# Awaiting the output's landing on the scalar engine instead of the sync engine

## The chip, the cores and the metric

The kernel runs on one core of one Trainium2 chip. The metric is device time in microseconds (us). Every execution also leaves a profile, whose span runs from the first to the last instruction of the program. The time is longer than the span (420.02 against 418.7 us in the kernel before), and the trace still records updates of semaphores up to 1.42 us after the span's end.

Five engines have instruction streams of their own: tensor (PE), vector (DVE), scalar (ACT), GpSimd (POOL) and sync (SP, which starts the DMAs here: all 46 of the trace before). Of that trace's 11609 instructions PE has 10472 (with the weight loads), DVE 715, ACT 330, POOL 40 and SP 52. In this kernel they wait for one another through semaphores (sync, for one, 40.6 us for vector's last cast before it starts the output DMA).

## The reference, cut to what matters

One decoding step of a block: modulation of the input, grouped attention over a cache of 32,768 positions, a projection, then a small MLP. All weights and both caches have to be read from HBM (178.28 MB in the profile); the output is 2 x 1 x 1024 bf16, 4 KB.

```python
def reference(A_x, A_k_cache, A_v_cache, A_wq, A_wo, B_x, B_w1, B_b1, B_w2, B_b2, c, w_mod):
    # ... _A_ref: q = x @ wq; softmax(q k^T) v over the cache; @ wo
    # ... _B_ref: layernorm, w1, gelu, w2
    # ...
    h = _layernorm(x, axis=-1) * (1 + cb) + sb
    x = x + gb * _B_ref(h, B_w1, B_b1, B_w2, B_b2)
    return x
```

## The kernel before

The kernel records the operations of each engine with the semaphore waits that they need, and emits them in one block, one section for each engine. At the end of the block all engines meet in a closing barrier. The change and the argument touch only the last lines of the kernel:

```python
    # ... (the whole computation is recorded above)
    dve(lambda e: e.tensor_copy(res16[:, :], psM[0:16, 0:128]), reads=["psM"], writes=["res16", "c16"])

    s_out = nc.alloc_semaphore("s_out")
    T.wait("sp", reads=["res16"])
    T.raw("sp", lambda e: e.dma_start(out.rearrange("b o (k p) -> (b o k) p", p=128), res16[:, :]).then_inc(s_out, 16))

    with nc.Block(no_gpsimd_drain=True) as block:
        T.emit(block)              # the sections of the engines, then the closing barrier
    nc.sync.wait_ge(s_out, 16)     # behind the barrier: the output DMA has landed
```

The output DMA is started by sync inside the block, and sync waits for its sixteen increments behind the barrier, so that the barrier runs while the DMA is in flight (in the trace the barrier lets the engines go between 418.09 and 418.15 us, and the DMA's increments come from 418.53 to 418.69).

## Time and profile before

| | kernel before |
|---|---|
| time, median of 3 runs | 419.99 us (419.98 to 420.00) |
| span of the profiled run (its time) | 418.7 us (420.02) |
| read from HBM | 178.28 MB, 426 GB/s |

The page of the profile, cut to the lines that say what bounds the kernel (the DMA row gives the mean busy share of the DMA engines in tenths, in 40 equal slices of the span):

```profile
span 418.7 us, 11609 instructions
...
DMA  9989999999999999999999999999999999899995
...
HBM read 178.28 MB, written 0.00 MB: 426 GB/s over the span
## 4 chain that ended last, share of the span: by engine, by line
DMA 71%; PE 24%; DVE 2%; issue 1%; ACT 1%; SPq 1%
```

The DMA engines are busy to the end: 0.99 of the time up to 417.3 us. The change can't touch that; it touches what comes after. The same kernel in order of time, its last two microseconds (start, duration, engine, line, operation):

```profile
417.03 0.28 DVE L736 CAST c<-psM 16x128 bf16<-16x128 f32 x1 [0.37 <-PE psM L734]
417.34 0.35 SPq L740 DMA_DIRECT2D out_dram<-c  x1
```

And what sync's queue waited for, same kernel (line, releaser, us in total, times, longest):

```profile
SPq L740 <- DVE c L736: 40.6, 1, 40.6
...
SPq L744 <- DMA out_dram<-c: 0.6, 1, 0.6
SPq L742 <- PEq L742: 0.2, 1, 0.2
```

L742 is the closing barrier, L744 the wait behind it. The single instruction at L744, before (engine, operation, duration in ns, first and last start in us):

```profile
L744 SPq EVENT_SEMAPHORE  x1: 17/17/17, 418.7 to 418.7; - x1
```

Read together with the semaphore records of the trace (in us from the span's start): the cast ends at 417.31, sync has started the output DMA by 417.69, the barrier lets every engine go between 418.09 and 418.15, the DMA's last increment is recorded at 418.69, and sync's wait starts at 418.707 and ends at 418.724. That is the end of the span. So the last thing in the program is a wait of 0.6 us for a DMA in flight, with all other engines done.

### The profile page before, as it was taken

The numbers are of one execution on the slowest core, as the hardware profiler recorded it, in microseconds if no ns is written. First come the engines' busy times: TensorE is split into PE (matmuls) and PEld (weight loads), VectorE is DVE, ScalarE is ACT, GpSimd is POOL, SyncE is SP. The second block draws the span as 40 slices with busy tenths as digits, with TensorE's granted clock in tenths as the row PEclk, the third lists the DMA queues.
The fourth block names the chain that finished last, engine by engine and source line by source line (L and its number), as shares of the span: only waits on it lengthen the run. The fifth ranks groups of instructions, "written<-read, shape, count | busy, mean of one in ns | idle before, by whom it ended". The sixth has DMA issues, their size and how long they took to land.

```text
span 418.7 us, 11609 instructions
## 1 busy us (share of the span) xinstructions
PE 291.0 (70%) x5183; PEld 231.3 (55%) x5183; DVE 209.6 (50%) x423; ACT 149.4 (36%) x179; POOL 6.8 (2%) x29
## 2 busy tenths in 40 slices
PE   1407449766996895699369957976995699564536
PEld 1104219762993794299149926962894399221214
DVE  1201105546677676467726664766477567620411
ACT  2000015533565364256405632643365166400100
POOL 3000000000000000000000000000000000000000
PEclk9999557986896997799589958986697889576585
DMA  9989999999999999999999999999999999899995
GB/s 373 450 380 449 448 404 493 398 406 446 441 432 429 423 451 429 419 454 457 391 435 476 407 416 448 438 438 426 438 438 426 416 460 457 377 448 428 424 427 249
DMA packets 5581, 178.42 MB, mean 426 GB/s; under 512 B 698, under 2 KB 706, under 8 KB 964
## 3 DMA queue, kind: packets, MB, share of 16 engines
q1 hardware_dynamic: 5572, 178.28, 98.8%
q8 instruction: 8, 0.13, 0.1%
q14 instruction: 1, 0.01, 0.0%
HBM read 178.28 MB, written 0.00 MB: 426 GB/s over the span
## 4 chain that ended last, share of the span: by engine, by line
DMA 71%; PE 24%; DVE 2%; issue 1%; ACT 1%; SPq 1%
DMA V<-in_A_v_cache_dram 39%; DMA wo<-in_A_wo_dram 10%; DMA K<-in_A_k_cache_dram 10%; PE psZ L584 10%; DMA w<-in_B_w_dram 9%; PE psKT L536 8%; DMA wmod<-in_w_mod_dram 4%; PE psS L548 1%; PE psZ L548 1%; PE psS L655 1%; PE psZ L729 1%; PE psZ L469 1%; ACT KT_sb L540 0%; PE psS L469 0%; DVE m1c L553 0%
## 5 line engine op out<-in xcount | busy, mean ns | idle before, releaser
L536 PE MATMUL psKT<-ident,K 128*128 128x128 bf16 x2048 | 163.1, 229 | 11.5 <-DMA K<-in_A_k_cache_dram 11.5
L540 ACT ACTIVATE KT_sb<-psKT 128x1024 bf16<-128x1024 bf16 x96 | 98.2, 1025 | 124.4 <-PE psKT L536 124.4
L542 DVE COPY KT_sb<-psKT 128x1024 bf16<-128x1024 bf16 x160 | 106.7, 688 | 61.6 <-PE psKT L536 61.2
L536 PEld LDWEIGHTS psKT<-ident,K 128*128 128x128 bf16 x2048 | 126.7, 102 | 13.0 <-DMA K<-in_A_k_cache_dram 12.7
L584 PE MATMUL psZ<-V,E_sb 128*32 128x512 bf16 x512 | 46.4, 541 | 23.2 <-DMA V<-in_A_v_cache_dram 20.0
L548 PE MATMUL psS<-qcur,KT_sb 128*128 128x8 bf16 x1024 | 44.7, 167 | 2.2 <-issue 2.2
L584 PEld LDWEIGHTS psZ<-V,E_sb 128*32 128x32 bf16 x512 | 18.7, 130 | 47.7 <-issue 38.8
L548 PE MATMUL psZ<-qcur,KT_sb 128*128 128x8 bf16 x1024 | 43.0, 167 | 2.2 <-issue 1.5
L548 PEld LDWEIGHTS psS<-qcur,KT_sb 128*128 128x128 bf16 x1024 | 40.0, 97 | 2.3 <-issue 2.3
L548 PEld LDWEIGHTS psZ<-qcur,KT_sb 128*128 128x128 bf16 x1024 | 37.9, 96 | 3.4 <-issue 1.6
L572 ACT ACTIVATE E_sb<-S_sb 128x512 bf16<-128x512 f32 x32 | 19.5, 630 | 29.6 <-DVE S_sb L570 29.6
L570 DVE TENSOR_TENSOR S_sb<-S_sb,gmb 128x512 f32<-128x512 f32 x32 | 20.0, 685 | 0.3
L576 DVE TENSOR_REDUCE rs<-E_sb 128x8 f32<-128x512 bf16 x32 | 19.7, 675 | 0.0
L469 PE MATMUL psS<-wmod,inT 128*32 128x512 bf16 x32 | 5.1, 624 | 16.2 <-DMA wmod<-in_w_mod_dram 16.2
L553 DVE TENSOR_REDUCE m1c<-psZ 128x8 f32<-128x512 f32 x16 | 11.1, 693 | 10.2 <-ACT S_sb L552 10.1
L595 DVE RECIPROCAL rinv<-psM 128x1 f32<-128x1 f32 x8 | 1.3, 168 | 27.7 <-PE psM L593 27.7
L605 PE MATMUL psM<-msum,hmat 128*128 128x128 f32 x16 | 4.2, 347 | 13.3 <-DVE msum L600 13.3
L559 PE MATMUL psM<-identf,m 128*8 128x128 f32 x16 | 4.3, 369 | 13.1 <-DVE m L556 13.1
L553 DVE TENSOR_REDUCE m1c<-psS 128x8 f32<-128x512 f32 x16 | 11.1, 693 | 3.2 <-ACT S_sb L552 3.1
L552 ACT ACTIVATE S_sb<-psZ 128x512 f32<-128x512 f32 x16 | 9.5, 595 | 7.5 <-PE psZ L548 7.5
L477 DVE COPY S_sb<-psS 128x512 f32<-128x512 f32 x1 | 0.7, 690 | 22.9 <-PE psS L469 22.9
L469 PEld LDWEIGHTS psS<-wmod,inT 128*32 128x32 bf16 x32 | 1.1, 132 | 19.3 <-DMA wmod<-in_w_mod_dram 18.0
(123 smaller groups left out, 167.5 us busy)
## 6 DMA issues: line engine op xcount, KB each, us to landing
K<-in_A_k_cache_dram SPq DMA_DIRECT2D x16, 4096.0 KB, 27.1
wq<-in_A_wq_dram SPq DMA_DIRECT2D x2, 4096.0 KB, 44.8
wo<-in_A_wo_dram SPq DMA_DIRECT2D x2, 4096.0 KB, 39.0
w<-in_B_w_dram SPq DMA_DIRECT2D x2, 3584.0 KB, 32.5
wmod<-in_w_mod_dram SPq DMA_DIRECT2D x1, 6144.0 KB, 29.8
w<-in_B_w_dram SPq DMA_DIRECT2D x3, 2048.0 KB, 37.8
wmod<-in_w_mod_dram SPq DMA_DIRECT2D x1, 4608.0 KB, 15.8
wmod<-in_w_mod_dram SPq DMA_DIRECT2D x1, 1536.0 KB, 6.0
```

What stands on the lines that cost most here:

```text
L469: pe(lambda e, w=it.view, k=k, kk=kk, ch=ch, n=n, q=q: e.matmul(bank[n][32 * q:32 * q + 32, :], lhsT=inT[:, k, :], rhs=w[:, kk, ch * 512:( ...
L536: pe(lambda e, kq=kq, jj=jj, w=kt, t=t: e.transpose(psKT[kq][:, jj * 128:(jj + 1) * 128], w[:, t, :], ident[:, :]), reads=[it.reg, "ident" ...
L540: act(lambda e, src=src: e.activation(KT_sb[g8][:, :, :], src, ACT.Copy), reads=[f"psKT{kq}"], writes=[f"KT_sb{g8}"], sem=f"ev{cc}_{g8}")
L542: dve(lambda e, src=src: e.tensor_copy(KT_sb[g8][:, :, :], src), reads=[f"psKT{kq}"], writes=[f"KT_sb{g8}"], sem=f"ev{cc}_{g8}")
L548: pe(lambda e, t=t, jj=jj: e.matmul(ps[:, t * HPG:(t + 1) * HPG], lhsT=KT_sb[g8][:, jj, :], rhs=qcur[:, :], start=True, stop=True), reads= ...
L552: act(lambda e: e.activation(Sc, ps.rearrange("p (t h) -> p h t", h=HPG), ACT.Copy), reads=[preg], writes=[f"S_sb_{cc}"], sem=f"sc{cc}")
L553: dve(lambda e: e.tensor_reduce(m1c[:, :, cc], ps.rearrange("p (t h) -> p h t", h=HPG), AX.X, ALU.max), reads=[preg], writes=[f"m1c{cc}"])
L559: pe(lambda e: e.matmul(psM[0:HPG, 0:128], lhsT=m1[:, :], rhs=identf[:, :], start=True, stop=True), reads=["m1", "identf"], writes=["psM"])
L570: dve(lambda e: e.tensor_tensor(Sc, Sc, gmb[:, :].unsqueeze(2).to_broadcast([128, HPG, TPC]), ALU.subtract), reads=[f"S_sb_{cc}", "gmb"], ...
L572: act(lambda e: e.activation(Ec, Sc.rearrange("p h (u t) -> p u h t", t=4), ACT.Exp, scale=SCALE), reads=[f"S_sb_{cc}"], writes=[f"E_sb_{c ...
L576: dve(lambda e: e.tensor_reduce(rs4[:, :, cc], Ec.rearrange("p u h t -> p h u t"), AX.XY, ALU.add), reads=[f"E_sb_{cc}"], writes=[f"rs4_{c ...
L584: pe(lambda e, t4=t4, tg=tg, q=q: e.matmul(psO[32 * q:32 * q + 32, :], lhsT=E_sb[:, tg // 4, :, :].rearrange("p h t -> p (h t)"), rhs=vt[: ...
```

## The change

The wait for the output is moved to another engine. It stays behind the barrier; the DMA, its issuer and its semaphore stay. The intent can be read as taking the wait from the engine that has just started the DMA and giving it to one that has been idle for 16 us.

```diff
     with nc.Block(no_gpsimd_drain=True) as block:
         T.emit(block)
-    nc.sync.wait_ge(s_out, 16)
+    nc.scalar.wait_ge(s_out, 16)
```

## The prediction

In the recorded texts a serpentine is a row of nine increments of one semaphore, taken as a walk through the five engines and back, and the postamble is what follows the program's last instruction. The trace's records hold the time of an update and the number of its semaphore, not the value and not the engine: which update is an increment, which a reset, and which engine makes it, is my reading, which the runs with other waiters test.

> **What bounds the kernel now.** Memory traffic, not the tail. The profile's page has a span of 418.7 us with DMA at 9 tenths in nearly every slice, 426 GB/s on average, and a chain that ended last of 71% DMA and 24% PE. The change touches only the last microsecond. There the trace, in order of time, has: DVE's last cast ends at 417.31; the sync engine issues the output DMA from 417.34 to 417.69; the closing barrier (semaphore instructions at L742) releases every engine between 418.09 and 418.15; the output DMA's sixteen increments arrive from 418.53 to 418.69; sync's wait at L744 starts at 418.707 and takes 17 ns. So sync really waits 0.6 us (the view of waits says the same), all of it the DMA's flight.
>
> **What the change removes, adds, moves.** One wait (17 ns) leaves sync's stream and one enters the scalar engine's. Scalar's last work is the sigmoid at 402.24, and the barrier releases it when it releases sync. The DMA, its issuer and its semaphore stay, so the wait should again end at about 418.72. Span: 418.7 within 0.1.
>
> [...] The profiled run's time, 420.02, is 1.30 us longer than its span. The trace's semaphore-update records show what follows the kernel: nine increments of one semaphore (418.387, .421, .631, .676, .841, .885, .923, .957, 419.004), then resets of all semaphores in five runs until 419.56, then nine increments again until 420.14. [...] From the order of the reset runs I read sync as the turning point, reached last on the way up, and scalar as the second. In the kernel before, four increments are made while sync still waits (the fifth at 418.841, 117 ns after the wait's end). With scalar held instead, only the first is early; the third, fourth and fifth, hidden before, come after scalar's. Estimate from the undisturbed serpentine at the trace's end (323 ns from second increment to ninth): scalar leaves its wait at 418.72, takes 117 ns (as sync) to at most 311 ns (its bound now) to its increment, and 323 ns later the ninth falls at 419.17 to 419.36 instead of 419.004. That is +0.16 to +0.35 us (0.04 to 0.08%), all on the critical path, since resets and the second serpentine follow.
>
> **Prediction.** 420.2 us, 8 times in 10 between 419.6 and 420.9. Chances: faster by over 2%: 0.01; within 2%: 0.98; slower by over 2%: 0.01.
>
> **What would show each step.** The wait stands on scalar and ends within 20 ns of the last increment; the span stays at 418.7 within 0.1; time minus span grows from 1.30 to about 1.5 us; the second increment (not the fifth) comes after 418.72, the rest follow at about 40 ns. The stream (426 GB/s, 71% DMA) is unchanged.
>
> **What would make it wrong.** If scalar is at the serpentine's turn, the effect is zero or slightly negative. If scalar's path from its last instruction into the postamble is longer than 311 ns once it starts late, the loss is larger. If two builds differ in the 418.7 us of traffic by a few tenths, that hides the effect; the three runs of before agree within 0.02 us, but are one build.

## The result, and the profile after

| | before | after |
|---|---|---|
| time, median of 6 runs | 420.01 us (419.98 to 420.09) | 420.32 us (420.26 to 420.40) |
| time, mean of the 6 | 420.023 | 420.323 |
| profiled run: time / span, from the trace | 420.02 / 418.724 | 420.29 / 418.749 |
| time minus span of the profiled run | 1.296 | 1.541 |

The ratio of the two kernels is 1.0007, 95% interval 0.9994 to 1.002. At a threshold of 2% the two kernels are the same, and the interval includes 1. Yet all six runs of after lie above all six of before, by 0.30 us in the mean. The page after:

```profile
span 418.7 us, 11609 instructions
...
DMA  9989999999999999999899999999999999899995
...
HBM read 178.28 MB, written 0.00 MB: 426 GB/s over the span
## 4 chain that ended last, share of the span: by engine, by line
DMA 79%; PE 18%; issue 1%; DVE 1%; SPq 1%; ACT 1%
```

The stream is the same. The chain's split is not (79% DMA instead of 71%), though nothing before the last microsecond was changed and the span is the same: in the kernel before it follows mostly matmuls from 104.9 to 138.0 us, and after the change a transfer from 100.1 to 130.4 us. A change in its shares alone proves nothing. In order of time, after:

```profile
417.05 0.28 DVE L736 CAST c<-psM 16x128 bf16<-16x128 f32 x1 [0.37 <-PE psM L734]
417.36 0.35 SPq L740 DMA_DIRECT2D out_dram<-c  x1
```

What sync's queue waited for, after; the wait at L744 is gone from it:

```profile
SPq L740 <- DVE c L736: 40.5, 1, 40.5
...
SPq L742 <- PEq L742: 0.2, 1, 0.2
```

And the instruction at L744, after, now on scalar's queue:

```profile
L744 ACTq EVENT_SEMAPHORE  x1: 17/17/17, 418.7 to 418.7; - x1
```

The last increment of the DMA is at 418.711, scalar's wait at 418.732 to 418.749. Up to here the two kernels differ by 0.025 us, and the wait itself costs 17 ns on either engine. The time came after the span, where the views of the profile show nothing; the trace's records of semaphore updates do. This is what they hold of one semaphore (number 2, which no instruction of the program names), in us from the end of the last wait (the span's end), so that the traces can be laid over each other:

```
first row of nine        1      2      3      4      5      6      7      8      9
before (sync held)   -0.337 -0.303 -0.093 -0.048 +0.117 +0.161 +0.199 +0.233 +0.280
after (scalar held)  -0.341 +0.125 +0.163 +0.207 +0.231 +0.336 +0.376 +0.411 +0.457

second row of nine      10     11     12     13     14     15     16     17     18
before               +1.062 +1.097 +1.135 +1.178 +1.202 +1.301 +1.339 +1.373 +1.420
after                +1.243 +1.346 +1.384 +1.428 +1.451 +1.550 +1.588 +1.622 +1.669
```

In between, from 0.12 us after the fifth increment in both traces, come single updates of semaphores numbered 7 to 255 in five rising runs (226 records from 418.961 to 419.562 us before, 245 from 419.095 to 419.768 after), which I read as resets. Two things grew. In the first row, only one increment instead of four is made while the wait lasts, and the ninth comes 0.177 us later (0.457 - 0.280). In the second row, the eleventh follows the tenth after 0.103 us instead of 0.035, which adds another 0.07. Together the eighteenth comes 0.249 us later, and time minus span grew by 0.245.

### The profile page after: what moved, and what is told of

Its sections match the earlier page's. It is cut to its first block, busy times and chain, and to the rows that moved or that the text cites. A ratio compares the mean times of both kernels' runs of the same rounds, so it can differ in the third digit from the quotient of the medians.

```text
span 418.7 us, 11609 instructions
## 1 busy us (share of the span) xinstructions
PE 290.7 (69%) x5183; PEld 231.0 (55%) x5183; DVE 209.7 (50%) x423; ACT 149.4 (36%) x179; POOL 6.8 (2%) x29
## 4 chain that ended last, share of the span: by engine, by line
DMA 79%; PE 18%; issue 1%; DVE 1%; SPq 1%; ACT 1%
DMA V<-in_A_v_cache_dram 46%; DMA K<-in_A_k_cache_dram 10%; DMA wo<-in_A_wo_dram 10%; PE psZ L584 10%; DMA w<-in_B_w_dram 9%; PE psKT L536 4%; DMA wmod<-in_w_mod_dram 4%; PE psS L655 1%; PE psS L548 1%; PE psZ L729 1%; PE psZ L548 1%; PE psZ L469 1%; PE psS L469 0%; SPq L647 0%; ACT KT_sb L540 0%
## 5 line engine op out<-in xcount | busy, mean ns | idle before, releaser
L655 PE MATMUL psS<-wo,atT 128*32 128x512 bf16 x64 | 7.0, 614 | 8.3 <-DMA wo<-in_A_wo_dram 8.3
L477 DVE COPY S_sb<-psS 128x512 f32<-128x512 f32 x1 | 0.7, 691 | 23.0 <-PE psS L469 23.0
L664 DVE COPY S_sb<-psS 128x512 f32<-128x512 f32 x2 | 1.4, 691 | 21.6 <-PE psS L655 14.6
```

Source lines behind the costliest of these rows:

```text
L655: pe(lambda e, w=it.view, m=m, j=j, hf=hf, q=q: e.matmul(psS[0][32 * q:32 * q + 32, :], lhsT=atT[m][:, j, :], rhs=w[:, j, hf * 512:(hf + 1 ...
```

## The experiments

The theory is that nine increments are a walk through the five engines and back, in a fixed order. A held engine early in the order delays more of the walk. There are four rivals: A, sync should hold the wait; B, chance differences between builds; C, scalar alone is slow to leave a wait; D, an instruction more in scalar's stream costs, held or not.

The differences are some tenths of a microsecond of 420. At the threshold of 2% every run is the same as the kernel before, and only w_pool, in_sp and in_act have a 95% interval of the ratio that lies above 1. Two finer measures are used: the traces' increments as above, and the mean of time minus span over all runs (spans are listed to 0.1 us, so one value is good to 0.05). For the kernel before that mean was 1.30, 1.29 and 1.30 in the three sets of runs below, each on one chip (9, 9 and 7 runs). All runs were correct.

| run | waits behind the barrier | median us (before, same set) | time minus span, mean | increment 9 | gap 10 to 11 | increment 18 |
|---|---|---|---|---|---|---|
| before (profiled) | sync | - | 1.30 | +0.280 | 0.035 | +1.420 |
| after | scalar | 420.32 (420.01) | 1.54 | +0.457 | 0.103 | +1.669 |
| both | sync and scalar | 420.33 (420.08) | 1.55 | +0.456 | 0.119 | +1.687 |
| w_dve | vector | 420.27 (420.08) | 1.43 | +0.402 | 0.034 | +1.546 |
| w_pe | tensor | 420.43 (420.08) | 1.60 | +0.564 | 0.034 | +1.704 |
| w_pool | GpSimd | 420.72 (420.08) | 1.88 | +0.831 | 0.034 | +1.974 |
| w_act | scalar | 420.25 (420.05) | 1.55 | +0.457 | 0.108 | +1.675 |
| idle_act | sync; scalar's is fulfilled | 420.12 (420.05) | 1.38 | +0.279 | 0.115 | +1.500 |
| in_sp | sync's is fulfilled | 420.91 (420.05) | 1.76 | +0.746 | 0.034 | +1.888 |
| in_act | scalar's is fulfilled | 421.09 (420.05) | 1.84 | +0.734 | 0.107 | +1.950 |
| idle4 | sync; scalar's are fulfilled | 420.34 (420.16) | 1.50 | +0.280 | 0.034 | +1.410 |
| idle8 | sync; scalar's are fulfilled | 420.09 (420.16) | 1.33 | +0.294 | 0.034 | +1.435 |
| idle_in | sync | 420.32 (420.16) | 1.51 | +0.279 | 0.034 | +1.415 |
| act_m1 | scalar | 420.47 (420.16) | 1.63 | +0.457 | 0.034 | +1.723 |

### Which engine is held: both, w_dve, w_pe, w_pool

```diff
# both                                # w_dve
     nc.sync.wait_ge(s_out, 16)      -    nc.sync.wait_ge(s_out, 16)
+    nc.scalar.wait_ge(s_out, 16)    +    nc.vector.wait_ge(s_out, 16)
# w_pe                                # w_pool
-    nc.sync.wait_ge(s_out, 16)      -    nc.sync.wait_ge(s_out, 16)
+    nc.tensor.wait_ge(s_out, 16)    +    nc.gpsimd.wait_ge(s_out, 16)
```

Expected of both:

> The wait on the output stands on the sync engine and on the scalar engine. Theory ([...] scalar is second, sync fifth): the earlier engine in the order decides, so this is the changed kernel again: time 0.25 to 0.35 us over the kernel before, second increment at about 0.125 us after the scalar wait's end, ninth at about 0.46 us after it. Rival A (the sync engine should be kept busy or the move itself, fewer instructions on sync, costs): within 0.1 us of the kernel before. Rival B (chance difference between two builds): anything within 0.3 us.

Expected of w_dve:

> The wait stands on the vector engine alone. Theory: vector is fourth in the serpentine, so only sync's hop and the turn come after it: increments 1 to 3 early, the fourth about 0.12 us after the wait's end, the ninth about 0.37 us after it (0.12 + 0.024 + 0.105 + 0.040 + 0.035 + 0.046) against 0.28 in the kernel before and 0.457 in the changed one: time +0.09 us over the kernel before, 0.05 to 0.2. Rival C (scalar alone is slow to leave a wait): within 0.05 us of the kernel before.

Expected of w_pe:

> The wait stands on the tensor engine alone. Theory: tensor is first, so no increment at all before the wait's end; its own path from its last instruction to its increment is 0.235 us in both traces, then 0.034 to scalar and 0.332 from scalar's to the ninth: ninth about 0.60 us after the wait's end, time +0.32 to 0.45 us over the kernel before (its wait instruction takes 51 ns, not 17). Rival C: within 0.05 us of the kernel before.

Expected of w_pool:

> The wait stands on GpSimd alone. Theory: third in the order, but its own path from its last instruction to its increment was 0.567 us in the kernel before (it came last of the first four there), so increments 1 and 2 early, third about 0.567 us after the wait's end, ninth about 0.86 us after it: time +0.5 to 0.65 us over the kernel before. If position alone counts and not the path: +0.15 us. Rival C: within 0.05 us.

Each wait stands where it was meant to. The instruction in w_dve, w_pe and w_pool, in this order (PEldq and DVEq are the queues of tensor and vector):

```profile
L744 DVEq EVENT_SEMAPHORE  x1: 21/21/21, 418.8 to 418.8; - x1
```

```profile
L744 PEldq EVENT_SEMAPHORE  x1: 51/51/51, 418.8 to 418.8; - x1
```

```profile
L744 POOLq EVENT_SEMAPHORE  x1: 17/17/17, 418.9 to 418.9; - x1
```

The first row of increments in their traces, in us from the wait's end:

```
                   1      2      3      4      5      6      7      8      9
w_pe (tensor)   +0.198 +0.232 +0.270 +0.314 +0.338 +0.444 +0.484 +0.518 +0.564
after (scalar)  -0.341 +0.125 +0.163 +0.207 +0.231 +0.336 +0.376 +0.411 +0.457
w_pool (GpSimd) -0.346 -0.311 +0.537 +0.581 +0.604 +0.710 +0.750 +0.784 +0.831
w_dve (vector)  -0.358 -0.324 -0.114 +0.156 +0.179 +0.282 +0.321 +0.356 +0.402
before (sync)   -0.337 -0.303 -0.093 -0.048 +0.117 +0.161 +0.199 +0.233 +0.280
```

This shows the order without any guess: with tensor held no increment is made during the wait, with scalar one, with GpSimd two, with vector three, with sync four. A held engine's own increment comes 0.117 (sync), 0.125 (scalar), 0.156 (vector), 0.198 (tensor) and 0.537 us (GpSimd) after its wait, and from there the walk takes its usual steps. In the means of the times (420.101 for the kernel before) three fell as expected: vector +0.13 us (420.230; 0.05 to 0.2 expected), tensor +0.36 (420.462; 0.32 to 0.45 expected), GpSimd +0.62 (420.716; 0.5 to 0.65 expected). The run both was a little under, +0.23 (420.330) or +0.25 in the medians, where 0.25 to 0.35 was expected; its increments came where they were expected. For vector, tensor and GpSimd the paths were each estimated 0.03 to 0.04 us off: the ninth increment was expected at 0.37, 0.60 and 0.86 and came at 0.402, 0.564 and 0.831. With both held, the result is that of scalar alone, not of sync. Rival A falls with that, and rival C with the other three: each engine but sync costs something.

### The same change again, and an instruction on scalar that is not held: w_act, idle_act

```diff
# w_act: the changed kernel          # idle_act
-    nc.sync.wait_ge(s_out, 16)      +    nc.scalar.wait_ge(T.sem['d_it0'], 16)
+    nc.scalar.wait_ge(s_out, 16)         nc.sync.wait_ge(s_out, 16)
```

Expected of w_act:

> The changed kernel again, unaltered, as the yardstick on the chip that runs the next three. Theory: +0.25 to 0.35 us over the kernel before, second increment after the wait's end, and in the second serpentine a gap of about 0.10 us before its second increment again. Rival B (chance difference between two builds or runs): anything within 0.3 us of the kernel before.

Expected of idle_act:

> The wait on the output stays on sync; scalar gets, at the same place behind the barrier, a wait that was fulfilled hundreds of microseconds before (the first weight load). Theory: one instruction more on scalar costs nothing when it is not held, since scalar has slack there: within 0.05 us of the kernel before, fifth increment after the wait's end. Rival D (one instruction more in scalar's stream, [...] is the cost): +0.2 to 0.3 us.

The repetition on another chip gave +0.20 us in the medians and in the means (420.254 against 420.052), a little under what was expected; in time minus span it gave 1.55 against 1.29, and its increments are those of after to within 4 ns in the first row and 7 ns in the second. So the tail repeats; chance differences in the 418.7 us before it account for the rest. Rival B falls for the tail.

In idle_act scalar's instruction ends at 418.29, long before sync's wait (418.805), as the two lines of its profile show:

```profile
L744 ACTq EVENT_SEMAPHORE  x1: 17/17/17, 418.3 to 418.3; - x1
```

```profile
L745 SPq EVENT_SEMAPHORE  x1: 17/17/17, 418.8 to 418.8; - x1
```

Its first row is that of the kernel before (ninth at +0.279). But the gap of 0.115 in the second row is there, and time minus span is 0.09 over the kernel before (the mean time 0.11). My expectation of "within 0.05 us" was wrong: rival D is right about this smaller part, and wrong about the larger one.

### Nobody held behind the barrier: in_sp, in_act

```diff
# in_sp and in_act: wait inside the block, ahead of the closing barrier
+    T.raw("sp", lambda e: e.wait_ge(s_out, 16))
     with nc.Block(no_gpsimd_drain=True) as block:
         T.emit(block)
# in_act besides
-    nc.sync.wait_ge(s_out, 16)
+    nc.scalar.wait_ge(s_out, 16)
```

Expected of in_sp:

> Sync waits for the output inside the block, ahead of the closing barrier, and again behind it as in the kernel before. The barrier then closes about 1.0 us later, as its last arrival moves from 417.92 to about 418.92, and nothing overlaps the DMA's flight: span +0.4 us, ninth increment at about 419.9 instead of 419.0, time +0.8 to 1.0 us over the kernel before. Wait behind the barrier already fulfilled.

Expected of in_act:

> As the run in_sp, but the wait behind the barrier stands on scalar. Theory (scalar costs more only because it is held when the others have arrived): now nobody is held behind the barrier, so scalar and sync are equal: within 0.05 us of in_sp. Rival D (the instruction on scalar costs by itself) and rival A (sync without it costs): in_act 0.2 to 0.3 us over in_sp.

In in_sp sync now waits for the DMA at the barrier's line (L743 in this file), and longer, since no barrier overlaps it:

```profile
SPq L743 <- DMA out_dram<-c: 1.0, 1, 1.0
...
SPq L743 <- PEq L743: 0.2, 1, 0.2
```

The span grew to 419.15, the ninth increment came at 419.897 (419.9 expected), the time by 0.87 us (means 420.922 and 420.052). That is what the place behind the barrier is worth. In in_act the first row is as in in_sp (ninth at +0.734 and +0.746): with nobody held, it no longer matters for that row which engine has the wait. The gap of 0.107 in the second row stays, and with it +0.08 in time minus span over in_sp (0.12 in the means of the times). So "within 0.05 us" was missed again, and by the same small part.

### What the small part depends on: idle4, idle8, idle_in, act_m1

The gap 10 to 11 had been 0.103 to 0.119 in all five kernels with one instruction more on scalar (after, both, w_act, idle_act, in_act) and 0.034 or 0.035 in all others. By its trace scalar executes 330 instructions in the kernel before and 331 in those; the expectations count instructions of the compiled program instead, 60 and 61. Four more kernels changed that number or the place of the extra instruction:

```diff
# shortened. idle4 (332 executed on scalar) with 4, idle8 (334) with 8: two waits to an instruction
+    for _ in range(4): nc.scalar.wait_ge(T.sem['d_it0'], 16)
     nc.sync.wait_ge(s_out, 16)
# idle_in (332): extra instructions inside the block
+    for _ in range(3):
+        T.raw("act", lambda e: e.wait_ge(T.sem['d_it0'], 16))
     with nc.Block(no_gpsimd_drain=True) as block:
# act_m1 (329): the changed kernel, a copy at the start goes from scalar to vector
-        if n == 1:
+        if n == 99:
             act(lambda e, dst=dst, n=n: e.activation(dst, bank[n][:, :], ACT.Copy), ...)
```

Expected of idle4:

> Four fulfilled waits on scalar behind the barrier, which the compiler packs two to an instruction: two instructions more on scalar than in the kernel before (62 against 60; idle_act had 61). The output is awaited on sync as before. What is looked at is the gap between first and second increment of the second serpentine: 35 ns in the kernel before, 103 to 119 ns in the five kernels with 61 on scalar. Theory E (a cost per instruction): about 190 ns (twice the 75 to 80 extra). Theory F (the length of scalar's stream shifts where its postamble falls, by parity): 35 ns again. Theory G (any length over 60): 105 to 120 ns. First serpentine as in the kernel before, ninth increment 0.28 us after the wait's end, in all three.

Expected of idle8:

> Eight fulfilled waits on scalar, four instructions more (64). Theory E: gap of about 350 ns, time +0.3 us over the kernel before. Theory F (parity): 35 ns. Theory G: 105 to 120 ns, time +0.1 us. A mixture, such as 35 here and 110 in idle4, would say that the place matters in steps larger than two.

Expected of idle_in:

> One fulfilled-wait instruction more on scalar (61), but inside the block, at the end of scalar's section, well ahead of the closing barrier, instead of behind it. If the stream's length is what matters (F or G): gap in the second serpentine of 105 to 120 ns as in idle_act. If it is an instruction between the barrier and the postamble that costs: 35 ns as in the kernel before. First serpentine as in the kernel before.

Expected of act_m1:

> The changed kernel (output awaited on scalar alone) with scalar's stream shortened to 59 instructions: one copy at the start of the kernel goes from scalar to vector, with its table load. The copy's move may shift the start by some tenths of a microsecond, so the trace's tail counts, not the time. Held-engine theory: second increment about 0.125 us after the wait's end, ninth 0.457 us after it, as in the changed kernel. Second serpentine: G (length over 60) and E: gap 35 ns; F (parity): 105 to 120 ns. If 35 ns, the last increment falls at 1.60 us after the wait's end instead of 1.67.

The expectation of idle_in counted one instruction more than before. Its trace has two, as many as idle4, since the third wait stands on a branch of its own:

```profile
L743 ACTq EVENT_SEMAPHORE  x1: 38/38/38, 402.5 to 402.5; - x1
...
L744 ACTq COMPARE_BRANCH  x1: 38/38/38, 402.6 to 402.6; - x1
```

The copy in act_m1 took no table load along: scalar has 12 there as before. The gap 10 to 11 was 0.034 in all four, and none of the three theories holds: not E (a cost per instruction) and not G (any length over 60), which wanted a larger gap in idle4 and idle8, and not F, the parity, since act_m1 was to have the gap. But a stop turned up somewhere else in each of them:

- idle8 (334): between increments 1 and 2 of the first row, 0.185 instead of 0.034. The walk still waits for sync there, and the fifth increment comes at +0.116 as before, so nothing of this stop is left. The 0.014 by which the ninth is late arises from the eighth, scalar's second in this row, which comes 0.013 late.
- idle4 (332, behind the barrier) and idle_in (332, inside the block): in one of the five runs of resets, that of semaphores 54 to 104, which I take for scalar's from its place. It starts 0.639 and 0.638 after the wait's end instead of 0.333. The second row is that of the kernel before, yet the time is longer: time minus span is 1.50 and 1.51 instead of 1.30.
- act_m1 (329): between increments 16 and 17, 0.157 instead of 0.034. The first row is that of the changed kernel to the nanosecond at the ninth (+0.457), so the large part doesn't come from the extra instruction.

So scalar makes a stop after the program's last instruction that comes earlier the more instructions precede it: with 329 it falls between increments 16 and 17, with 331 between 10 and 11, with 332 ahead of scalar's resets, with 334 between 1 and 2. The two kernels with 332 agree though one has the extra instructions ahead of the barrier, so by these two it is their number that counts, not their place. With 330, the kernel before, no stop is seen; by this sequence it would fall between 11 and 16, where scalar waits for the others anyway, but that isn't shown.

The trace shows where the stop falls and that it moves with the stream; it doesn't show its cause. One kind of record goes with it. After the program's end the DMA queue that the profile calls "instruction" moves a packet of 8192 bytes in idle4, idle8 and idle_in, and in none of the other eleven traces. In idle4 (window from 418.7 to 421 us):

```profile
q14 instruction: 1, 0.01, 1.5%
```

From idle4 and idle8 to the kernel before only scalar's stream differs, so this packet goes with its length. But it starts 0.65 to 1.0 us after the stop is over (1.292, 0.854 and 1.285 us after the last wait's end in idle4, idle8 and idle_in), the record doesn't name its engine, and no run changed this transfer alone. So whether it has to do with the stop isn't shown.

For 11 of the 14 traces the time ends 0.11 to 0.13 us before the eighteenth increment, reckoned from the span's end, as in before (1.420 - 1.296) and after (1.669 - 1.541). In act_m1 it is 0.08, in idle_in 0.02, and in idle4 the time ends 0.20 after it. In idle4 and idle_in the packet above lands last, 1.841 (1.292 + 0.549) and 1.627 (1.285 + 0.342) after the span's end, and the time ends 0.233 and 0.234 before that; in idle8 it lands at 1.309 (0.854 + 0.455), ahead of the eighteenth increment, and the time ends as in the 11. So in those two the time seems to end with the packet, which no run tested. For act_m1 it is open.

No kernel had a shorter time minus span than the one before (the median of idle8 is 0.07 us lower, but by its spans, while its tail is longer). If nobody were held at all, the walk would wait for GpSimd's increment (0.093 before the wait's end in the trace before), and the ninth would come 0.294 later as in w_pool, at +0.201 instead of +0.280. So the kernel before is within an estimated 0.08 us of anything that another waiter could give.

## Why the prediction was right, point by point

- **Bound by memory traffic, unchanged by the change.** Right: 426 GB/s and a span of 418.7 in both. That the chain would stay at 71% DMA was wrong (79%), without any bearing on the time.
- **The wait costs the same on scalar, and the span stays.** Right: 17 ns on both, spans of 418.724 and 418.749. Scalar's wait began 21 ns after the last increment, sync's 16 ns.
- **The walk's order: tensor, scalar, GpSimd, vector, sync, and back.** It was read from the order of the reset runs; the four kernels with other waiters show the way up, and the way back is my reading of the last four increments. The undisturbed row that ends the trace of the kernel before took 358 ns (1.420 - 1.062); hop by hop it shows 24 to 43 ns on the way up, then 99 ns, then 34 to 47 ns.
- **Scalar's path from its wait to its increment, estimated at 0.117 to 0.311 us.** It took 0.125, and the walk from there 0.332 (0.323 predicted). The ninth increment came 0.177 us later from the wait's end, 0.202 in absolute terms (419.206 against 419.004); 0.16 to 0.35 was predicted.
- **All of it on the critical path.** Right: the tenth increment moved from +1.062 to +1.243, by 0.181.
- **The term that was missing from the sum.** Time minus span was to grow to "about 1.5"; it grew to 1.54. The difference is scalar's stop before the eleventh increment, 0.103 instead of 0.035, which adds about 0.07 us. It comes from the extra instruction in scalar's stream and is there when scalar is not held (idle_act, in_act). The prediction left it out, as it treated the moved instruction itself as 17 ns, and that the growth came so near to "about 1.5" is in part luck: the walk alone gave 0.18 of it. The time of 420.32 against 420.2 predicted is made of this, of 0.025 us in the span of the profiled runs, and of the scatter of single runs. The range of 419.6 to 420.9 would have held with no effect at all (420.01), so the hit in time says little; the increments are what tested the mechanism.

In sum: 0.177 (the walk) and about 0.07 (scalar's stop) make the 0.249 by which the eighteenth increment moved from the span's end; with the 0.025 of the span that is the 0.27 between the two profiled runs (420.29 - 420.02). That the first part is caused by the holding and not by the instruction is shown by idle_act and in_act, where it vanishes, and by act_m1, where it stays with a shorter stream.

## What to carry to other kernels

In this kernel the last wait is not free of the engine it stands on: after the program the engines are collected in a fixed order (the increments show it), and the wait for the landing cost least on the engine that is collected last on the way up (sync, against +0.13 us on vector, +0.25 on scalar, of which about 0.07 is its stop, +0.30 on tensor and +0.58 on GpSimd in time minus span). The place in the order isn't all: GpSimd is third, and costs most by its own long path (0.537 us from its wait to its increment). The wait belongs behind the closing barrier here (0.87 us less than ahead of it). Each of these is about 0.2% of 420 us or less, so it may be worth a line in a short kernel, which wasn't tried, and nothing in a long one. For effects of this size compare time minus span and the records of the tail, since the times of whole runs scatter by as much as the effect (0.28 us in nine runs of the kernel before on one chip, 419.93 to 420.21).
